# A list-building router beside linear attention: router steps, breaks on GpSimd and late gathers are moved

## The chip, the cores and the metric

The kernel runs on one core of one Trainium2 chip. The metric is the time of one execution on the device in microseconds. Three runs of the kernel before and one profiled execution of it are at hand. Everything is in fp32.

## The reference, cut to what matters

A gated linear attention (4 batches, 8 heads, 768 steps, 48 columns per head) is computed first. Its output, turned to 3072 tokens of 384 columns, goes through a router that picks 2 of 8 experts for each token, and through these experts.

```
f = 1 / (1 + exp(-f_logit))
for t in range(S):
    state = f[t] * state + k[t] (x) v[t]
    y[t] = q[t] . state
x = y as (3072, 384)
noisy = x @ w_gate + log1p(exp(x @ w_noise)) * noise
top2 = the two largest of noisy;  weights = softmax over the two
out[token] += weight * (relu(x[token] @ w1[e]) @ w2[e])      for both experts e
```

## The kernel before

**Attention stage.** The 768 steps are cut into 6 chunks (NCH) of 128 for each of the 4 batches, 24 blocks in all, which are done in 12 groups `g` of two blocks. Queries, keys and gates come in through a ring of buffers. TensorE turns q and k (`turn_q`, `turn_k`), makes the scores of the two blocks (`scores`, s = 0 and 1), VectorE masks them (A, L589), TensorE multiplies them with v (`within`), adds the carried state (`before`), turns the output into token rows (`features`), which SP stores to `x_rows` in DRAM. GpSimd multiplies and adds the carried state (`carried`: mid and st).

**Router and lists.** As soon as a chunk's logits are there, `route(c)` computes the two experts, their weights, and the place of each token in its expert's list. It is a generator: between its short VectorE, ScalarE and TensorE operations it yields, and the main loop takes a step or a few of it in each of its slots, so that a step's place in the engines' program order is set by the number of yields before it. The slots have names: "sc0" and "sc1" come after the two score halves, "y0" and "y1" after the two products with v. At the end of `route` there are 8 scatters for the chunk (`put`, L733), each an indirect DMA from GpSimd (POOL) that writes 128 list entries to `lists` in DRAM; 48 scatters in all. The main loop pops them one at a time. After each, `breath` puts a memset into POOL's queue: a tiny one (`spacer`), or, after every third, a break: a memset of one partition that is long in columns. In the chunks c = 0 to 4 (`c <= HALF + 1`, with HALF = 3) breaks are made; chunk 5 has none. In chunks 0 to 2 a break covers 2048 columns, later 768 and 576.

**Experts.** The work is cut into 10 items. Items 0 and 1 are the first 256 list entries (one "pair" of two blocks of 128) of experts 0 and 1; they use lists that are filled by chunks 0 to 2 and start within the attention stage. Items 2 and 3 are two further pairs of experts 1 and 0, items 4 to 9 three pairs each of experts 2 to 7. For each pair p:

- `fetch`: SP reads 256 list entries (4 KB) into `slots`. From pair 2 on this waits for all 48 scatters to land.
- `gather`: two indirect DMAs of POOL (s = 0 and 1, 128 rows each) read the token rows from `x_rows` into `xg` (4 buffers).
- For items 4 to 9, `stored` writes the 256 rows (384 KB) back to DRAM and `laid` reads them in another layout (4 DMAs of 96 KB), both on SP; then VectorE turns 32 x 32 blocks (STREAM_TRANSPOSE, L945). For the other items TensorE turns the rows (`xgp`, L949).
- the first layer, 8 pieces for each item (L1027 or L1166), the second layer, 7 pieces for each pair (y, L1332), and two scatters of POOL that add to the output (L1213). The turns for the next item sit in the second layer of the item ahead of it, in `between`.

The weights of an item (w1 and w2, 1.5 MB each) are loaded by SP; so are the weights for five further small blocks ("quarters", `w_q`, 1.5 MB for a load). The order on each engine is the order in which the program was written out, for SP and POOL too; `ahead(what, until)` issues the next fetches, stores, re-layouts and gathers up to a bound, from the loop over `pieces` at the end. Scatters of a pair wait for those of the pair ahead to land, since they add to the same rows.

In the second half of the kernel, a gather of a whole pair is issued at even pieces, wherever a pair's slots have been fetched, so some gathers stand between the scatters of the item that runs.

Of the kernel before, what the change touches and what calls it, by code (L numbers as in the profile page):

```python
# [332 lines left out]
def kernel(  # L333
# [94 lines left out]
    def two_banks(name):  # L428
        return ps2.tile([128, 2, 512], F32, tag="two", name=name)
# [142 lines left out]
    def turn_k(g, s):  # L572
        if s == 0:
            kT[g] = wk.tile([128, 2, HP * C], F32, tag="kT", name=f"kT_{g}")
            kT[g, "p"] = two_banks(f"kp_{g}")
        turn(kT[g, "p"][:, s], "k", g, s)
        if g == 0:
            nc.vector.tensor_copy(kT[g][:, s], kT[g, "p"][:, s])
        elif s == 1:
            nc.vector.tensor_copy(kT[g], kT[g, "p"])  # L580

    def scores(g, s):
        sc = sc_of[g, s] = two_banks(f"sc_{g}_{s}")
        for hp in range(HP):
            for par in range(2):
                nc.tensor.matmul(sc[:, par, cols(hp)], lhsT=kT[g][rows(par), s, cols(hp)],  # L586
                                 rhs=qT[g][rows(par), s, cols(hp)], start=True, stop=True)
        A[g, s] = wk.tile([C, 2, HP * C], F32, tag="A", name=f"A_{g}_{s}")
        nc.vector.tensor_tensor(A[g, s].rearrange("j r (a i) -> j (r a) i", i=C), sc.rearrange("j r (a i) -> j (r a) i", i=C),  # L589
                                causal.unsqueeze(1).broadcast_to((C, H, C)), ALU.mult)  # L590

    def carried(g):
# [11 lines left out]
        if c:  # L604
            mid = wk.tile([128, 2 * HP, D], F32, tag="mid", name=f"mid_{g}", bufs=1)
            nc.gpsimd.tensor_tensor(mid, ds, state[g % 2], ALU.add)
            ds = mid
        nc.gpsimd.tensor_tensor(new, ds, last, ALU.mult)
        state[g % 2] = new

# [47 lines left out]

    xs_of = {}

    def route(c):
# [26 lines left out]
        nc.vector.tensor_tensor(ex, mx[:, :, 0:2], mx[:, :, 0:1].broadcast_to((128, B, 2)), ALU.subtract)  # L688
        for _ in range(2):
            yield from pause()  # L690
# [19 lines left out]
        else:  # L710
# [3 lines left out]
                                     data1=each.rearrange("t e b -> t (e b)"), initial=0.0, op0=ALU.mult, op1=ALU.add)  # L714
        for _ in range((4, 5, 5, 17, 11, 8)[c]):
            yield from pause()
# [14 lines left out]
        def put(b, r):  # L731
            n_put.append(c)
            into = nc.gpsimd.indirect_dma_start(  # L733
                out=lists, out_offset=bass.IndirectOffsetOnAxis(ap=sloti[:, r, b:b + 1], axis=0),
                in_=entry[:, c, b, r, :], in_offset=None)
            tc.declare_no_dep(into.ins, group="lists", reason="slots differ")
            tc.add_to_no_dep_group("lists", into.ins)
            if c >= HALF:
                tc.declare_no_dep(into.ins, group="full", reason="slots differ")
                tc.add_to_no_dep_group("later", into.ins)  # L740
            breath(c <= HALF + 1)

        puts.extend([partial(put, b, r) for b in range(B) for r in range(2)])
        yield


    in_a_row = [0]

    def breath(broken):
# [3 lines left out]
        elif len(n_put) <= HALF * B * 2:  # L753
            nc.gpsimd.memset(spare[0:1, :], 0.0)
        else:
# [917 lines left out]
    for i in range(-3, NG):  # L1673
        for what in chain(back(i), front(i)):
# [17 lines left out]
            elif i == NG - 1 and what in ("x0", "x1", "f"):  # L1692
                zeros(4)
            for _ in range(6 if n_routed == NCH else 2 if n_routed == HALF + 1 else 3 if n_routed == NCH - 1 and i == NG - 1 else 1):
                next(router, None)
# [16 lines left out]
            if what == ("L0" if through(i + 2) or i == NG - 1 else "y1") and (i >= 2 and i % 2 == 0 or i == NG - 1):  # L1712
# [6 lines left out]
                if c == NCH - 1:  # L1719
                    router = chain(router, plan(), beyond())  # L1720
        if i < 0:
            warm_up(4)
# [19 lines left out]
    for item, piece in pieces:  # L1742
# [4 lines left out]
        if piece % 2 == 0 or item < NE - 1 and piece > 8:  # L1747
            ahead("laid", first_of[min(item + 2, len(items))])
            ahead("stored", done["gather"])
            ahead("gather", min(done["gather"] + 1, p + 4 if item < NE - 1 else first_of[min(item + 2 + (item >= NE), len(items))]))  # L1750
        n = item - NE - 2
# [60 lines left out]
```

## Time and profile before

| | |
|---|---|
| three runs | 620.51, 620.44, 618.16 us; median 620.44 |
| profiled execution | 621.6 us, span 619.8 us |
| TensorE (PE) busy | 599.9 us, 97% of the span |
| VectorE (DVE) | 455.8 us, 74% |
| ScalarE (ACT) | 279.8 us, 45% |
| GpSimd (POOL) | 246.8 us, 40% |
| mean granted TensorE clock | 0.989 of full speed |

The span runs from the first to the last instruction of the profile; the execution's own time has 1.8 us around it. A busy TensorE is not one at its peak: each fp32 matmul takes several passes. The span falls into the attention stage (to about 145 us), the first two items (to 195) and the other items.

### The profile page before, as it was taken

The numbers are of one execution on the slowest core, as the hardware profiler recorded it, in microseconds if no ns is written. First come the engines' busy times: TensorE is split into PE (matmuls) and PEld (weight loads), VectorE is DVE, ScalarE is ACT, GpSimd is POOL, SyncE is SP. The second block draws the span as 40 slices with busy tenths as digits, with TensorE's granted clock in tenths as the row PEclk, the third lists the DMA queues.
The fourth block names the chain that finished last, engine by engine and source line by source line (L and its number), as shares of the span: only waits on it lengthen the run. The fifth ranks groups of instructions, "written<-read, shape, count | busy, mean of one in ns | idle before, by whom it ended". The sixth has DMA issues, their size and how long they took to land.

```text
span 619.8 us, 12902 instructions
## 1 busy us (share of the span) xinstructions
PE 599.9 (97%) x4767; PEld 539.3 (87%) x4767; DVE 455.8 (74%) x1032; ACT 279.8 (45%) x715; POOL 246.8 (40%) x260
## 2 busy tenths in 40 slices
PE   8999999999969999999999999999999999999995
PEld 7788888777959998998898899889988898998994
DVE  6559778776735758898887878778788877887840
ACT  5766665532113323247316621761374247317611
POOL 3213299898864342151153224322433152323032
PEclk9999999998988999999999999999999999999998
DMA  9999999969345679868866795769576949661024
GB/s 181 172 198 197 214 199 194 217 184 355 117 114 146 163 143 212 173 149 232 223 139 200 187 227 109 212 173 212 124 223 166 250 98 271 138 140 23 0 27 55
DMA packets 184511, 104.71 MB, mean 169 GB/s; under 512 B 144284, under 2 KB 177564, under 8 KB 184440
## 3 DMA queue, kind: packets, MB, share of 16 engines
q1 hardware_dynamic: 172392, 84.46, 53.4%
q0 software_dynamic: 12048, 19.35, 17.3%
q8 instruction: 39, 0.64, 0.4%
q14 instruction: 32, 0.26, 0.2%
HBM read 76.80 MB, written 27.23 MB: 168 GB/s over the span
## 4 chain that ended last, share of the span: by engine, by line
PE 79%; POOL 7%; DMA 7%; issue 2%; DVE 2%; SPq 1%; ACT 1%; POOLq 0%; ACTq 0%; DVEq 0%
PE y L1332 29%; PE D L1166 7%; PE E L1166 7%; PE C L1166 5%; PE B L1166 5%; POOL lists L733 5%; DMA out_dram<-ys,slots 2%; PE sc L617 2%; PE sc L586 2%; PE A L1166 2%; PE P L1027 2%; PE L L541 1%; SPq L523 1%; PE qp L563 1%; DMA xg<-x_rows,slots 1%
## 5 line engine op out<-in xcount | busy, mean ns | idle before, releaser
L1213 POOL DMA_INDIRECT out_dram<-ys,slots x48 | 79.9, 1664 | 175.5 <-DVE ys L1338 102.6
L1332 PE MATMUL y<-q_all,f_all 128*128 128x192 f32 x528 | 94.7, 327 | 1.4 <-ACT ys L1348 1.4
L1332 PEld LDWEIGHTS y<-q_all,f_all 128*128 128x128 f32 x528 | 86.6, 190 | 2.1 <-ACT ys L1348 1.7
L895 POOL DMA_INDIRECT xg<-x_rows,slots x48 | 49.5, 1032 | 72.7 <-DMA slots<-lists 31.9
L1332 PE MATMUL y<-w,hs_b 128*128 128x192 f32 x352 | 64.4, 326 | 0.0
L733 POOL DMA_INDIRECT lists<-entry,sloti x48 | 52.5, 1094 | 20.1 <-DVE mx L683 11.0
L1338 DVE SCALAR_TENSOR_TENSOR ys<-y,slots,ys 128x192 f32<-128x192 f32 x66 | 27.4, 415 | 44.2 <-PE y L1332 16.5
L1332 PEld LDWEIGHTS y<-w,hs_b 128*128 128x128 f32 x352 | 58.4, 190 | 0.4
L1174 ACT ACTIVATE hs_b<-hs_b 128x256 f32<-128x256 f32 x120 | 50.1, 418 | 8.3 <-DVE hs_b L1178 7.2
L1381 ACT ACTIVATE ys<-y,slots 128x192 f32<-128x192 f32 x22 | 9.3, 422 | 96.9 <-PE y L1332 96.9
L589 DVE TENSOR_TENSOR A<-sc,causal 128x1024 f32<-128x1024 f32 x24 | 28.7, 1219 | 12.3 <-PE sc L586 12.2
L1332 PE MATMUL y<-w,f_all 128*128 128x192 f32 x176 | 32.7, 329 | 0.0
L1332 PE MATMUL y<-q_all,hs_b 128*128 128x192 f32 x176 | 32.7, 329 | 0.0
L1332 PEld LDWEIGHTS y<-q_all,hs_b 128*128 128x128 f32 x176 | 28.9, 190 | 2.1 <-issue 2.1
L1201 DVE TENSOR_TENSOR f_all<-hs_b 128x512 f32<-128x512 f32 x44 | 30.0, 685 | 0.0
L1332 PEld LDWEIGHTS y<-w,f_all 128*128 128x128 f32 x176 | 28.9, 190 | 0.8
L1166 PE MATMUL C<-v_all,ws_b 128*128 128x256 f32 x96 | 28.7, 380 | 0.1
L586 PEld LDWEIGHTS sc<-qT,kT 64*128 64x128 f32 x384 | 22.5, 188 | 6.4 <-issue 3.5
L1171 ACT COPY hs_a<-D 128x256 f32<-128x256 f32 x66 | 24.5, 370 | 7.2 <-PE D L1166 5.4
L617 PEld LDWEIGHTS sc<-A,v_all 128*64 128x64 f32 x384 | 20.6, 137 | 6.2 <-DVE A L589 4.2
L617 PE MATMUL sc<-A,v_all 128*64 128x128 f32 x384 | 24.5, 277 | 1.0 <-DVE A L589 1.0
L586 PE MATMUL sc<-qT,kT 64*128 64x128 f32 x384 | 24.9, 279 | 0.6 <-DVE mx L683 0.6
(277 smaller groups left out, 1413.0 us busy)
## 6 DMA issues: line engine op xcount, KB each, us to landing
w<-in_moe_w_dram SPq DMA_DIRECT2D x40, 384.0 KB
w_q<-in_moe_w_dram SPq DMA_DIRECT2D x10, 1536.0 KB
w<-in_moe_w_dram SPq DMA_DIRECT2D x6, 1536.0 KB
rows_of<-xg SPq DMA_DIRECT2D x18, 384.0 KB
v_all<-in_v_dram SPq DMA_DIRECT2D x12, 384.0 KB
x_rows<-xs SPq DMA_DIRECT2D x12, 384.0 KB
out_dram<-zero SPq DMA_DIRECT2D x24, 192.0 KB
k_all<-rows_of SPq DMA_DIRECT2D x48, 96.0 KB
```

Source lines behind the costliest of these rows:

```text
L586: nc.tensor.matmul(sc[:, par, cols(hp)], lhsT=kT[g][rows(par), s, cols(hp)], rhs=qT[g][rows(par), s, cols(hp)], start=True, stop=True)
L589: nc.vector.tensor_tensor(A[g, s].rearrange("j r (a i) -> j (r a) i", i=C), sc.rearrange("j r (a i) -> j (r a) i", i=C), causal.unsqueeze( ...
L617: nc.tensor.matmul(at(g, s, h), lhsT=slot_of("v", g)[:, s, h, :], rhs=A[g, s][:, h % 2, cols(h // 2)], start=(j < 2), stop=(g < 2 and j >= ...
L733: into = nc.gpsimd.indirect_dma_start(out=lists, out_offset=bass.IndirectOffsetOnAxis(ap=sloti[:, r, b:b + 1], axis=0), in_=entry[:, c, b, ...
L895: nc.gpsimd.indirect_dma_start(out=xg[p][:, s, :], out_offset=None, in_=x_rows[0:HALF * B * C] if p < NE else x_rows, in_offset=bass.Indir ...
L1166: nc.tensor.matmul(banks[name, j], lhsT=half_of(x, k)[:, j * 128:(j + 1) * 128], rhs=half_of(y, k), start=first, stop=True, skip_group_che ...
L1171: nc.scalar.copy(at(to, j), banks[more[0], j])
L1174: nc.scalar.activation(at(to, j), at(y, j), AF.Relu, scale=-1.0 if more[0][0] == "-" else 1.0)
L1201: nc.vector.tensor_tensor(sm[which], x, y, op)
L1213: into = nc.gpsimd.indirect_dma_start(out=out, out_offset=bass.IndirectOffsetOnAxis(ap=slots[p][:, s, 2:3], axis=0), in_=ys[s], in_offset= ...
L1332: nc.tensor.matmul(to, lhsT=x[:, o, :], rhs=y[:, o, :], start=(start and o == 0), stop=(o == FH - 1), skip_group_check=not start)
L1338: nc.vector.scalar_tensor_tensor(to, in0=bank, scalar=gate[s], in1=to, op0=ALU.mult, op1=ALU.add)
```

## The change

Four things are changed. In the main loop the router takes no step in the slot "sc0", and twice the usual number in "y0"; in chunk 3 eight of its pauses are moved from after the running count to ahead of the exponential. Breaks: they are 1400 columns in chunks 0 to 2, chunk 5 has them too, and `carried` starts the count of three again. At the start, the two halves of the first group's turned keys get a bank each in place of one tile of two banks, and four warm-up matmuls are left out. In the loop over pieces, from item 2 on, a gather is issued by halves in pieces 1 to 8, one half for each piece, in place of a whole pair at even pieces.

```
     def turn_k(g, s):
         if s == 0:
             kT[g] = wk.tile([128, 2, HP * C], F32, tag="kT", name=f"kT_{g}")
-            kT[g, "p"] = two_banks(f"kp_{g}")
+            if g:
+                kT[g, "p"] = two_banks(f"kp_{g}")
+        if g == 0:
+            p = one_bank(f"kp_0_{s}")
+            turn(p, "k", 0, s)
+            nc.vector.tensor_copy(kT[0][:, s], p)
+            return
         turn(kT[g, "p"][:, s], "k", g, s)
-        if g == 0:
-            nc.vector.tensor_copy(kT[g][:, s], kT[g, "p"][:, s])
-        elif s == 1:
+        if s == 1:
             nc.vector.tensor_copy(kT[g], kT[g, "p"])
...
         nc.gpsimd.tensor_tensor(new, ds, last, ALU.mult)
+        in_a_row[0] = 0
         state[g % 2] = new
...
-        for _ in range(2):
+        for _ in range(10 if c == HALF else 2):
             yield from pause()
         nc.scalar.activation(ex, ex, AF.Exp)
...
-        for _ in range((4, 5, 5, 17, 11, 8)[c]):
+        for _ in range((4, 5, 5, 9, 11, 8)[c]):
             yield from pause()
...
-            breath(c <= HALF + 1)
+            breath(True)
...
         elif len(n_put) <= HALF * B * 2:
-            nc.gpsimd.memset(spare[0:1, :], 0.0)
+            nc.gpsimd.memset(spare[0:1, 0:1400], 0.0)
...
-            for _ in range(6 if n_routed == NCH else 2 if n_routed == HALF + 1 else 3 if n_routed == NCH - 1 and i == NG - 1 else 1):
+            steps = 2 if n_routed == HALF + 1 else 3 if n_routed == NCH - 1 and i == NG - 1 else 1
+            for _ in range(6 if n_routed == NCH else 0 if what == "sc0" else 2 * steps if what == "y0" else steps):
                 next(router, None)
...
-        if i < 0:
+        if i < -1:
             warm_up(4)
...
         if piece % 2 == 0 or item < NE - 1 and piece > 8:
             ahead("laid", first_of[min(item + 2, len(items))])
             ahead("stored", done["gather"])
-            ahead("gather", min(done["gather"] + 1, p + 4 if item < NE - 1 else first_of[min(item + 2 + (item >= NE), len(items))]))
+        if item >= NE:
+            if 1 <= piece <= 8 and done["gather"] < min(done["fetch"], first_of[min(item + 3, len(items))]):
+                gather(done["gather"], (1 - piece % 2,))
+                done["gather"] += 1 - piece % 2
+        elif piece % 2 == 0 or item < NE - 1 and piece > 8:
+            ahead("gather", min(done["gather"] + 1, p + 4 if item < NE - 1 else first_of[item + 2]))
```

## Rows read from the trace of the kernel before

**Rows 1.** The page: the busy time of each engine, and the group of the list scatters (count | busy us, mean ns of one | idle us before them).

```profile
PE 599.9 (97%) x4767; PEld 539.3 (87%) x4767; DVE 455.8 (74%) x1032; ACT 279.8 (45%) x715; POOL 246.8 (40%) x260
...
L733 POOL DMA_INDIRECT lists<-entry,sloti x48 | 52.5, 1094 | 20.1 <-DVE mx L683 11.0
```

**Rows 2.** The waits of TensorE, the longest in total: what waited, for whom, us in total, times, longest us.

```profile
PE xgp L949 <- DMA xg<-x_rows,slots: 6.6, 2, 5.2
```

**Rows 3.** Windows: from:to and length in us, then the busy time of PE, PEld, DVE, ACT and POOL (with instructions), the mean granted TensorE clock, the share of the DMA engines, GB/s.

```profile
0.00:27.00 27.00, 24.67 (x266) 20.39 (x268) 15.39 (x30) 16.34 (x31) 4.96 (x24) 1.00 0.91 178
...
136.00:146.00 10.00, 8.67 (x97) 6.39 (x96) 4.38 (x16) 2.38 (x6) 8.79 (x14) 0.83 0.84 254
...
180.00:191.00 11.00, 6.03 (x27) 5.94 (x28) 1.38 (x4) 1.77 (x5) 5.49 (x5) 0.69 0.95 302
191.00:600.00 409.00, 407.53 (x2559) 375.14 (x2558) 324.48 (x704) 180.29 (x501) 125.03 (x92) 1.00 0.67 161
```

**Rows 4.** The chain that ended last, around the second pair's gather: start us, us, what.

```profile
172.78 4.71 DMA lists<-entry,sloti
177.51 2.73 DMA slots<-lists
...
181.03 3.80 DMA xg<-x_rows,slots
...
184.97 0.87 PE xgp L949 x3
```

**Rows 5.** The timeline of POOL in the first half of the list scatters (start us, us, engine, line, operation, out<-in; in brackets the idle time before it and what ended it): a scatter, a break and the scatter behind it, and scatter 25.

```profile
96.53 0.96 POOL L733 DMA_INDIRECT lists<-entry,sloti  x1 [0.22 <-issue]
97.48 1.79 POOL L754 MEMSET hs_a<- 1x2048 f32 x1
99.44 0.96 POOL L733 DMA_INDIRECT lists<-entry,sloti  x1 [0.17 <-issue]
...
129.11 1.54 POOL L733 DMA_INDIRECT lists<-entry,sloti  x1 [0.16 <-issue]
```

**Rows 6.** The same of chunks 4 and 5: scatters 38 to 41, 44 and 48, with a break between the first two.

```profile
158.21 1.01 POOL L733 DMA_INDIRECT lists<-entry,sloti  x1 [0.22 <-issue]
...
160.74 0.96 POOL L733 DMA_INDIRECT lists<-entry,sloti  x1 [0.17 <-issue]
...
162.01 0.96 POOL L733 DMA_INDIRECT lists<-entry,sloti  x1 [0.22 <-issue]
...
163.27 0.96 POOL L733 DMA_INDIRECT lists<-entry,sloti  x1 [0.22 <-issue]
...
167.06 1.63 POOL L733 DMA_INDIRECT lists<-entry,sloti  x1 [0.22 <-issue]
...
172.78 2.52 POOL L733 DMA_INDIRECT lists<-entry,sloti  x1 [0.23 <-issue]
```

**Rows 7.** The timeline of VectorE: the casts that end the routing of chunks 3 and 5, and two subtractions of weights.

```profile
123.78 0.17 DVE L729 CAST sloti<-slot 128x8 uint32<-128x8 f32 x1 [0.18 <-DVE slot L728]
...
155.54 0.17 DVE L729 CAST sloti<-slot 128x8 uint32<-128x8 f32 x1
...
172.06 0.94 DVE L974 TENSOR_TENSOR q_all<-w,q_all 128x768 f32<-128x768 f32 x1
...
173.53 0.94 DVE L974 TENSOR_TENSOR q_all<-w,q_all 128x768 f32<-128x768 f32 x1
```

**Rows 8.** The timeline of TensorE: the second half of group 9's products with v, which waits for its mask.

```profile
116.59 1.09 PE L617 MATMUL sc<-A,v_all 128*64 128x128 f32 x16 [0.69 <-DVE A L589]
```

**Rows 9.** The chain that ended last, at the start.

```profile
9.91 7.59 DMA k_all<-in_k_dram
...
20.61 5.55 DMA f_all<-in_f_logit_dram
```

**Rows 10.** Around TensorE's one stop among the late items, in item 7: two lines of the chain (the second layer's first products; a scatter to the output until it landed), and the timelines of SP (weight loads) and of TensorE.

```profile
468.77 2.60 PE y L1332 x16
...
482.06 10.61 DMA out_dram<-ys,slots
...
481.08 1.79 SPq L920 DMA_DIRECT2D w<-in_moe_w_dram  x4
...
483.45 0.40 SPq L1408 DMA_DIRECT2D w_q<-in_moe_w_dram  x1
...
493.33 1.57 PE L1332 MATMUL y<-q_all,f_all 128*128 128x192 f32 x8 [1.41 <-ACT ys L1348]
```

**Rows 11.** The timelines in item 5, which begins at 328 us: SP's two weight loads, POOL's last scatter of item 4 and the next gather, the start of the second layer on TensorE, and VectorE's transposes of item 6's first two pairs.

```profile
331.48 0.49 SPq L923 DMA_DIRECT2D w<-in_moe_w_dram  x1
...
332.65 0.38 SPq L1406 DMA_DIRECT2D w_q<-in_moe_w_dram  x1
...
342.71 1.57 POOL L1213 DMA_INDIRECT out_dram<-ys,slots  x1 [6.55 <-ACT hs_a L1171]
349.01 1.01 POOL L895 DMA_INDIRECT xg<-x_rows,slots  x1 [4.73 <-DMA slots<-lists]
...
354.10 1.46 PE L1332 MATMUL y<-w,hs_b 128*128 128x192 f32 x8
...
362.02 0.97 DVE L945 STREAM_TRANSPOSE xt_a<-k_all 128x768 f32<-128x768 f32 x1
...
367.33 0.97 DVE L945 STREAM_TRANSPOSE xt_a<-k_all 128x768 f32<-128x768 f32 x1
```

More of the change, by code (lines that the diff above doesn't have):

```diff
@@ L590, in scores @@
                                 causal.unsqueeze(1).broadcast_to((C, H, C)), ALU.mult)
+    in_a_row = [0]
     def carried(g):
@@ L657, in turned_logits @@
                                 p.rearrange("t s (r w) -> t s w r", r=HP)[:, :, 0:2 * E], axis=AX.X, op=ALU.add)
-    xs_of = {}
     def route(c):
@@ L740, in put @@
                 tc.add_to_no_dep_group("later", into.ins)
-            breath(c <= HALF + 1)
+            breath(True)
         puts.extend([partial(put, b, r) for b in range(B) for r in range(2)])
         yield
-    in_a_row = [0]
     def breath(broken):
```

## The prediction

> **What bounds the kernel now.** I read the page's busy times first. TensorE is busy 599.9 us of the 619.8 us span [rows 1], so an edit that shortens work on another engine can pay at most the 20 us in which TensorE stands still, and what its clock loses around those gaps. Next I read what TensorE waited for [rows 2] and the windows by stage [rows 3]. The attention stage starts with some gaps under its first loads. Then there are two sore places: 136 to 146 us, where 1.3 us are idle and the mean granted clock is 0.83 of full speed, and 180 to 191 us, where 5 us are idle and the clock is 0.69. From 191 to 600 us TensorE is idle only 1.5 us in 409. Its longest wait is for gathered rows (xg) [rows 2].
>
> Last I read the chain through the second sore place [rows 4]. Backwards: the transposes of pair 2 wait for the gather of its rows (3.80 us), that for its slots out of the lists (2.73), and that for the last list scatter to land: it starts at 172.78 us and lands 4.71 later, at 177.49. From there to TensorE's restart at 184.97 are 7.48 us that the change leaves alone. Before them POOL runs scatters and breaks end to end [rows 5, 6], from its first scatter to the 48th. So in this stage the time is set by POOL's queue, and what the change is worth here is how much earlier scatter 48 lands. TensorE cannot eat that up: it stands still 5.2 us before the restart [rows 2].
>
> **The first half's breaks.** I counted POOL's order through the loop for both versions. Before, chunks 0 to 2 have 8 breaks of 2048 elements. After, the counter starts again behind each carried state, so there are 6 breaks of 1400. A broken step takes 2.91 us from scatter to scatter (96.53 to 99.44 [rows 5]), an unbroken one 1.26 (162.01 to 163.27 [rows 6]), so a break costs 1.65. The memset is 1.79 us of it [rows 5]; at 1400/2048 of that, 1.22 (an estimate), a new break costs 1.08. POOL saves 8 x 1.65 - 6 x 1.08 = 6.7 us and could start scatter 25 at 122.4 us in place of 129.11. It may not: chunk 3's slots are written by VectorE only at 123.78 + 0.17 = 123.95 us [rows 7], and the change to chunk 3's pauses (8 fewer late, 8 more early) leaves that cast at the same place of VectorE's order. So scatter 25 starts at 124.0: **5.1 us earlier**, the rest is lost in a wait. Behind it POOL stays the bound: chunk 4's and 5's slots are early enough (chunk 5's at 155.7 [rows 7], its first scatter at 163.27 [rows 6], some 158 after).
>
> **The last chunk's breaks.** In chunk 5, scatters 41, 44 and 47 get a break. With one, a step takes 2.53 us (158.21 to 160.74), without 1.26 [rows 6], so three add **3.8 us**, straight in the chain. Two scatters of this chunk are long now: number 44 takes 1.63 us and number 48 takes 2.52, against 0.96, together 2.23 over. What breaks do to that no row of before shows. Bounds: all 2.23 stays, or all goes. While number 48 runs, VectorE does two subtractions of two SBUF operands, to 174.47 us [rows 7]; such overlaps come by chance of timing, and over all 48 scatters the mean is 1.09 us [rows 1], 0.13 over the usual, or 1.1 for eight. I take that mean, nearer to how such overlaps fall than either end: 2.2 becomes 1.1, **1.1 us gained**.
>
> The Trainium skill, "SBUF — State Buffer", in its section on the two sides of SBUF, says that VectorE and GpSimd share a port pair under an exclusive lock, which a VectorE instruction with two SBUF inputs takes against a GpSimd instruction that reads SBUF; whoever starts first holds it to its end. Number 48 fits it. By that rule a break, which only writes, could run while VectorE holds the pair, and the scatters behind it would be free of it: 2.2 gained in place of 1.1.
>
> **The router's steps.** Steps issued after the first half of the scores move behind the first half of the products, so that the second mask is not queued behind two maxima. That mask holds TensorE 0.69 us at 116.59 [rows 8]. It may bring chunk 3's slots, and so scatter 25, forward by 0 to 0.7 us; I take 0, since POOL's own queue is then close behind. Elsewhere the moved steps are short and wait for nothing new. The edits at the start (kp in two one-bank tiles, 4 fewer warm-up matmuls) cost and bring nothing: until 26 us the chain runs through loads, k of 7.59 us and f of 5.55 [rows 9]. Without that cover no more than the 2.3 us for which TensorE is idle there [rows 3] could be gained, and a lower clock after fewer warm-up matmuls could cost as much.
>
> The first gathers, of pair 0, also come 5.1 us earlier and take away the wait and the slow clock around 140 us (some 3 us of TensorE's time [rows 3]). That is worth nothing by itself: TensorE only comes earlier to the wait at 180 us. **List stage: 5.1 - 3.8 + 1.1 = 2.4 us, bounds 1.3 and 5.1 - 3.8 + 2.2 + 0.7 = 4.2.**
>
> **Late gathers by halves.** From item 2 on, gathers leave their places between the scatters and go into pieces 1 to 8 of the item before the one that uses them. The count of instructions and bytes is the same. On POOL the scatters no longer queue behind gathers that wait for slots (349.01, 4.73 us of waiting [rows 11]). What can that bring? TensorE is stopped once: at 493.33 for 1.41 us, by ScalarE, which waits for the buffer of a scatter issued at 482.06 [rows 10]. That one took 10.61 us to land, while SP had just issued two weight loads, at 481.08 and 483.45 [rows 10]. Before the first of them in SP's queue stands the re-layout of a pair that is gathered late. After the change it stands ahead of that and can go out when the first layer ends, at 468.77 [rows 10], 12 us earlier. **I take the 1.4 us as gained**; bounds 0 and 1.4.
>
> What is late next: SP's store and re-layout of each pair. SP now stores pair 12 (item 5, for instance) when item 5 has begun, and the weights for item 7 are issued ahead of the re-layout of pair 13. VectorE's transposes want the first pair at 362.02 and the second at 367.33, 7.9 and 13.2 us after the second layer begins at 354.10 [rows 11]. POOL's last scatter of the item before goes out at 342.71 now, 14 us into the item, with gathers in its way, so six gathers end there some 8 us later, and stores and re-layouts fill the rest. The re-layout of pair 13 waits for 1.5 MB of weights issued from 354.1 on. Two such loads and the slots behind them took 331.48 to 349.01 [rows 11], 8.8 us each; the re-layout's own 0.4 MB adds some 2 at that rate, so it lands near 366: a margin of about 1 us. I take no stall.
>
> The Trainium skill speaks against this part: "DMA: Bandwidth & Descriptors", section on queues, rings and completion order, has each DMA engine consume the descriptors of a ring in order, so small copies of SP wait out the weights before them. The 4.73 us wait of the gather at 349.01 for a 4 KB fetch agrees.
>
> **Sum:** 2.4 + 1.4 = 3.8 us off the profiled execution, 621.6 us (span 619.8): 617.8. Its own time is 1.2 us over the median of 620.44, so on that scale **616.6 us**. About 0.5%, 3.1 us, is what a measurement of this kernel tells from no change.
>
> **Rivals.** (a) *The last chunk's breaks eat the gain*: the long scatters stay long, POOL meets some in the first half too, and the gap at 493 us stays or moves. Gain 1.3 us or less: 619.1. For it: 3.8 of 5.1 us are certain costs on the chain. Against: a mean excess of 0.13 us. Chance 0.25. (b) *Late re-layouts stall VectorE and through it TensorE*, slower: items 4 to 8 turn pairs of a blocked item. The point is 13.2 us after the second layer's start; if the second re-layout lands 1.5 us behind it in each of the five, that is 7.5 us, less 2.4: 625.5. For it: the margin of 1 us. Against: weights and scatters go out earlier too, and now the first re-layout is done well before 362. Chance 0.15. (c) *The breaks shield the scatters*: they run beside VectorE's two-operand work, every scatter of chunk 5 is short, and the mask brings 0.7: 4.2 + 1.4 = 5.6 us, 614.8. For it: number 48. Against: a break is as likely to end in such work as to cover it. Chance 0.10. The lock of the Trainium skill's "SBUF — State Buffer" would make it so. My forecast has 0.50; its own range is 614.8 to 619.1.
>
> **Range and chances.** 613.0 to 621.0 us holds the forecast, (a) and (c), with 1.2 us for the spread of the runs before (618.16 to 620.51), and leaves out (b) and little else. Faster by over 0.5% means below 617.3: 0.36 of the forecast's 0.50, with (c) and some of the spread, 0.48. Slower: (b) and 0.01, 0.16. Between: 0.36.
>
> **What would show it.** Right: scatter 25 on POOL at 124 us, six memsets of 1400 at about 1.2 us, no wait on xg near 140; scatter 48 landing 2 to 3 us earlier and the restart 7.5 us behind it; scatters of chunk 5 at 0.96 us beside three breaks; no wait on a scatter's landing near 490. Wrong: scatter 25 held beyond 125 by chunk 3's slots or scatters that are long again; scatter 48 landing after 176; stream transposes waiting for re-laid rows, and TensorE gaps after 250 us.

## The result: half a per cent slower

The changed kernel takes 621.88 us (median of 22 runs), the kernel before 619.95 us beside it: a ratio of 1.0055, 95% interval 1.0037 to 1.0073. The medians are 1.9 us apart, the ratio makes 3.4 us: the ratios here and below leave out runs more than 1.5% above the fastest one of the same kernel (6 of 22 of the kernel before, none of the changed one), so they lie above the quotients of the medians, here 1.0031. The predicted range, to 621.0 us, doesn't reach the measured time. The profiled executions are 2.1 us apart (own time 623.72 us against 621.6, span 622.0 against 619.8).

The windows of the changed kernel, as in [rows 3]:

```profile
0.00:27.00 27.00, 24.35 (x264) 20.37 (x264) 15.91 (x30) 16.81 (x31) 4.97 (x24) 1.00 0.94 184
...
136.00:146.00 10.00, 10.00 (x120) 7.80 (x118) 6.22 (x24) 3.37 (x9) 8.68 (x15) 1.00 0.85 239
...
180.00:191.00 11.00, 7.62 (x38) 7.51 (x39) 1.62 (x5) 1.44 (x3) 4.86 (x5) 0.69 1.00 305
191.00:600.00 409.00, 404.14 (x2534) 371.35 (x2533) 322.67 (x699) 179.45 (x499) 127.00 (x92) 1.00 0.67 160
```

The sore place at 136 to 146 us is gone. The one at 180 is a little smaller (7.62 us busy against 6.03) and its clock is still 0.69. The loss stands in the last line: from 191 to 600 us TensorE is busy 404.14 us, where it was 407.53 [rows 3]. Its waits say for what (as in [rows 2]):

```profile
PE xgp L952 <- DMA xg<-x_rows,slots: 5.9, 1, 5.9
PE y L1335 <- DVE ys L1341: 4.7, 2, 3.2
PE rk L723 <- DVE each L710: 1.7, 1, 1.7
```

The second wait is new. Before, one stop of 1.41 us stood there [rows 10]; now there are two, and they cost 3.3 us more than it did. The third is new as well: TensorE waits for chunk 3's counts.

In the list stage, POOL's timeline answers to [rows 4 to 6]: a break of the first half, scatter 25, scatters 44, 47 and 48, the gather of pair 2; then TensorE's restart.

```profile
115.79 1.26 POOL L757 MEMSET hs_a<- 1x1400 f32 x1
...
125.42 1.01 POOL L738 DMA_INDIRECT lists<-entry,sloti  x1 [3.78 <-DVE sloti L734]
...
164.85 1.63 POOL L738 DMA_INDIRECT lists<-entry,sloti  x1 [0.22 <-issue]
...
170.54 2.55 POOL L738 DMA_INDIRECT lists<-entry,sloti  x1 [0.22 <-issue]
...
174.61 0.96 POOL L738 DMA_INDIRECT lists<-entry,sloti  x1 [0.17 <-issue]
...
179.38 1.00 POOL L898 DMA_INDIRECT xg<-x_rows,slots  x1 [1.61 <-DMA slots<-lists]
```

```profile
183.38 0.88 PE L952 MATMUL xgp<-ident,xg 128*128 128x128 f32 x3 [5.86 <-DMA xg<-x_rows,slots]
```

A short break takes 1.26 us (the estimate was 1.22). Scatter 25 starts 3.7 us earlier than before, not 5.1. Scatter 48 starts at 174.61, 1.8 us *later* than its 172.78 [rows 6], because three breaks stand ahead of it and the two long scatters are as long as they were (1.63 and 2.55; the second is now number 47). TensorE restarts at 183.38 in place of 184.97: 1.6 us earlier. So in the profiles 1.6 us are won, 3.3 us lost; that makes 1.7 of the 2.2 us between the two spans.

### The profile page after: what moved, and what is told of

Same layout as the page of the kernel before. It is cut to its first block, busy times and chain, and to the rows that moved or that the text cites. A ratio compares the mean times of both kernels' runs of the same rounds, so it can differ in the third digit from the quotient of the medians.

```text
span 622.0 us, 12895 instructions
## 1 busy us (share of the span) xinstructions
PE 598.0 (96%) x4759; PEld 538.0 (87%) x4759; DVE 460.2 (74%) x1032; ACT 280.0 (45%) x715; POOL 244.5 (39%) x263
## 5 line engine op out<-in xcount | busy, mean ns | idle before, releaser
L1216 POOL DMA_INDIRECT out_dram<-ys,slots x48 | 81.8, 1704 | 201.1 <-DVE ys L1341 122.4
L1335 PE MATMUL y<-q_all,f_all 128*128 128x192 f32 x528 | 94.3, 327 | 0.0
L1335 PEld LDWEIGHTS y<-q_all,f_all 128*128 128x128 f32 x528 | 86.7, 190 | 0.3
L1335 PE MATMUL y<-w,hs_b 128*128 128x192 f32 x352 | 64.4, 326 | 0.0
L1335 PEld LDWEIGHTS y<-w,hs_b 128*128 128x128 f32 x352 | 58.4, 190 | 0.4
L1335 PE MATMUL y<-w,f_all 128*128 128x192 f32 x176 | 33.0, 331 | 4.8 <-DVE ys L1341 4.7
L1335 PEld LDWEIGHTS y<-w,f_all 128*128 128x128 f32 x176 | 28.7, 190 | 6.5 <-DVE ys L1341 5.7
L1335 PE MATMUL y<-q_all,hs_b 128*128 128x192 f32 x176 | 32.7, 329 | 0.0
L1335 PEld LDWEIGHTS y<-q_all,hs_b 128*128 128x128 f32 x176 | 28.9, 190 | 2.1 <-issue 2.1
```

The lines of the kernel that those rows point to most:

```text
L1216: into = nc.gpsimd.indirect_dma_start(out=out, out_offset=bass.IndirectOffsetOnAxis(ap=slots[p][:, s, 2:3], axis=0), in_=ys[s], in_offset= ...
L1335: nc.tensor.matmul(to, lhsT=x[:, o, :], rhs=y[:, o, :], start=(start and o == 0), stop=(o == FH - 1), skip_group_check=not start)
```

## Experiments

Kernels were run on five chips, each time with the kernel before beside them; ratios are to that one. The kernel before took 616.9 to 619.0 us on three of the chips and 623 to 624 us on two. On these two, all profiles show idle time of TensorE that nothing in the trace ends, and several conclusions come out the other way; they are taken last, except for one kernel that is marked.

**The late gathers, both ways.** First the changed kernel with the old line for the gathers, and the kernel before with the new ones alone:

```
-        if item >= NE:
-            if 1 <= piece <= 8 and done["gather"] < ...
...
+            ahead("gather", min(done["gather"] + 1, p + 4 if item < NE - 1 else first_of[min(item + 2 + (item >= NE), len(items))]))
```

> The changed kernel with the late gathers put back as they were (whole pairs, where the kernel before had them); the router's steps, the pauses, the breaks stay changed. Theory 1 (the late gathers lose the time: two stops of TensorE for y, 3.16 + 1.54 us, in place of one of 1.41; the list stage gains 1.6): the two stops go, the one of 1.4 near 493 comes back, and the kernel is 1.6 us faster than the one before, about 618.3, ratio 0.997. Theory 2 (the loss sits in the router's steps and the breaks, the late stops are covered elsewhere): as slow as the changed kernel, 621.5 or more, ratio 1.003 to 1.006. Theory 3 (the stops in the late items move about with any shift of the stage before them): some stop for y of 1 to 5 us at another place, ratio 0.998 to 1.004.

> The kernel before with the late gathers by halves alone. Theory 1: the list stage is that of before (gather of the first late pair near 181.0, TensorE going on near 185.0), and the late items lose 4.70 - 1.41 = 3.3 us: about 623.2, ratio 1.005, with VectorE waiting for a re-laid pair 5 us near 483 to 490. Theory 2: the late items lose nothing, 618.5 to 620, ratio 0.998 to 1.000.

Measured: 618.8 us (kernel before 618.97; 1.0026, 0.9996 to 1.0055) without them, and 622.06 (1.0075, 1.0034 to 1.0115) with them alone. By medians the late gathers alone cost 3.1 us, near the 3.3 of the changed kernel's profile; between the changed kernel and the one without them the medians differ by 3.1 us too (not taken side by side; by the ratios it is 1.8 us). So theory 1 holds for its second half, by the times. Its first half doesn't: the rest of the change wins nothing. And the trace of the late gathers alone doesn't show 3.3 us. VectorE does wait for re-laid pairs in it, as theory 1 said, but TensorE loses no more by it than the 1.41 us of before, and in the window from 191 to 600 us it is busy 407.55 us, as it was (407.53 [rows 3]):

```profile
DVE xt_a L945 <- DMA k_all<-rows_of: 5.5, 2, 3.0
PE y L1332 <- DVE ys L1338: 1.4, 2, 1.0
```

So the loss is shown by the times of these runs; that it comes by VectorE's wait is read from the changed kernel's profile and is not shown for every run. Theory 3, stops that move about, isn't excluded either: its range holds the kernel without late gathers.

**What lies in the rest.** On that chip, two more kernels with old late gathers: breaks out of the last chunk again (`breath(c <= HALF + 1)`), and chunk 3's pauses back to 2 and 17.

> The changed kernel with old late gathers, and without the three breaks of 1.30 us in the last chunk's scatters. Theory 1: the breaks stand on POOL's path and shield nothing (the two long scatters of 1.63 and 2.55 us are there with them as without), so the first late gather comes 3.9 us earlier, near 175.5, and the time is 614 to 615, ratio 0.991. Rival (breaks shield the scatters): without them the eight scatters of the last chunk cost 2 to 4 us more, the gather is within 1.5 us of 179.4, and the time is within 1.5 us of the run with old late gathers.

> The changed kernel with old late gathers and chunk 3's pauses as before (2 ahead of the exponential and 17 ahead of the ranks, not 10 and 9). Theory 1: the new pauses make chunk 3's slots late (scatter 25 waited 3.78 us for them and began at 125.42); with the old ones it begins near 124.0, and the first late gather comes 1.4 us earlier: 617, ratio 0.995. Rival (scatter 25's start is made good by the slots of the later chunks): the gather stays near 179.4 and the time is that of the run with old late gathers, ratio 0.997.

Without the last chunk's breaks: 613.17 us (0.9929, 0.9903 to 0.9955), 5.6 us below the run that has them. POOL's timeline of that kernel, scatters 45 and 48, the scatter to the output and the gather of pair 2, and its window:

```profile
164.93 1.65 POOL L738 DMA_INDIRECT lists<-entry,sloti  x1 [0.22 <-issue]
...
169.42 0.96 POOL L738 DMA_INDIRECT lists<-entry,sloti  x1 [0.22 <-issue]
170.75 3.11 POOL L1216 DMA_INDIRECT out_dram<-ys,slots  x1 [0.29 <-issue]
174.22 1.01 POOL L898 DMA_INDIRECT xg<-x_rows,slots  x1 [0.37 <-issue]
```

```profile
180.00:191.00 11.00, 10.24 (x61) 9.54 (x61) 7.00 (x19) 3.08 (x7) 3.52 (x3) 1.00 0.75 207
```

Scatter 48 starts 5.2 us before that of the changed kernel (169.42 against 174.61) and the gather follows it 4.8 us behind in both. Three breaks of 1.30 us are 3.9 of the 5.2. The rest is the second long scatter: without breaks the list is finished when VectorE's subtractions (L977) come for the second time, and what is held then is the scatter to the output (3.11 us), behind the last list scatter. The breaks pushed scatter 47 into those subtractions. From 180 to 191 us TensorE now works 10.24 of 11 us at full clock. Theory 1's 3.9 us hold; that the long scatters stay on the list's path with breaks as without doesn't.

The old pauses: 619.86 us (1.0037, 1.0003 to 1.007), scatter 25 at 125.85 after a wait of 4.10 us. Theory 1 of that run falls; the pauses aren't what makes the slots late. Its TensorE stops twice for y among the late items, though it has the old late gathers (`PE y L1335 <- ACT ys L1351: 3.1, 2, 1.8`), so such stops do move. VectorE's and POOL's timelines of the changed kernel show what makes the slots late, and those of the kernel before (the last three lines) how it was:

```profile
119.08 1.69 DVE L693 TENSOR_TENSOR ex<-mx 128x8 f32<-128x8 f32 x1
121.04 0.62 DVE L699 SCALAR_TENSOR_TENSOR sm<-ex 128x4 f32<-128x4 f32 x1 [0.27 <-ACT ex L696]
```

```profile
118.72 0.96 POOL L738 DMA_INDIRECT lists<-entry,sloti  x1 [0.22 <-PE qp L563]
...
119.73 1.00 POOL L612 TENSOR_TENSOR mid<-ds,st 128x384 f32<-128x384 f32 x1
120.81 0.83 POOL L614 TENSOR_TENSOR st<-mid,ending 128x384 f32<-128x384 f32 x1
```

```profile
119.09 0.16 DVE L688 TENSOR_TENSOR ex<-mx 128x8 f32<-128x8 f32 x1
119.53 0.16 DVE L694 SCALAR_TENSOR_TENSOR sm<-ex 128x4 f32<-128x4 f32 x1 [0.28 <-ACT ex L691]
...
126.33 0.99 POOL L606 TENSOR_TENSOR mid<-ds,st 128x384 f32<-128x384 f32 x1
```

Two small instructions of the router, 0.16 us each in the kernel before, end with POOL's two operations for the carried state (120.77 with 120.73, 121.66 with 121.64). POOL's shorter breaks moved those operations under the router of chunk 3; before they came behind it, at 126 us. So chunk 3's slots are written at 125.1, not 123.95 [rows 7]. The run with old pauses shows the same two (1.69 and 0.62 us).

**Which part brings the gain.** The kernel before with one part each, in the order short breaks, router's steps with pauses, start:

```
-            nc.gpsimd.memset(spare[0:1, :], 0.0)
+            nc.gpsimd.memset(spare[0:1, 0:1400], 0.0)
```

```
+            steps = 2 if n_routed == HALF + 1 else 3 if n_routed == NCH - 1 and i == NG - 1 else 1
+            for _ in range(6 if n_routed == NCH else 0 if what == "sc0" else 2 * steps if what == "y0" else steps):
```

```
-        if i < 0:
+        if i < -1:
             warm_up(4)
```

> The kernel before with the shorter breaks of the first half alone, once more. On a chip where the kernel before takes about 619 us and TensorE has no unexplained idle time in the attention stage: Theory A (these breaks are the 5.8 us that the change gains beside its losses) 0.991 to 0.994; Theory B (scatter 25 is then held by chunk 3's slots, and it takes the router's steps too) 0.996 to 0.999. Where the kernel before takes 623 us or more: 1.003 to 1.007, as in the two runs there.

> The kernel before with the router's steps and chunk 3's pauses alone, once more. On a chip where the kernel before takes about 619 us: Theory A 0.999 to 1.001 (scatter 25 stays near 129), Theory B 0.996 or less. Where the kernel before takes 623 us or more: 1.000 to 1.007, as in the run there.

> The kernel before with the two edits at the start alone (banks of their own for the first two turned keys, and no filling products in the step before the first group). Theory A: the start waits for its first loads whatever TensorE does, so nothing: within 0.5 us of the kernel before. Theory B: the missing filling products leave TensorE's clock low for longer, 1 us or more slower; or the separate banks let the first group begin earlier, 1 us or more faster.

Short breaks alone: 612.54 us beside 616.93 (0.9944, 0.9909 to 0.9980). Router's steps alone: 615.22 us (0.9989, 0.9958 to 1.0020). Start alone, on one of the two chips taken last: 623.35 us beside 624.0 (1.0007, 0.9969 to 1.0046). The times lie nearest to theory A each time. POOL's timeline with the short breaks alone, scatters 25 and 48 and the gather:

```profile
124.81 1.00 POOL L736 DMA_INDIRECT lists<-entry,sloti  x1 [3.04 <-DVE sloti L732]
...
168.69 0.96 POOL L736 DMA_INDIRECT lists<-entry,sloti  x1 [0.22 <-issue]
...
173.82 1.01 POOL L897 DMA_INDIRECT xg<-x_rows,slots  x1 [0.68 <-issue]
```

Scatter 25 is 4.3 us earlier than in the profile of the kernel before, the gather 7.2, of which 5.7 come from scatter 48: it starts 4.1 us earlier, ahead of VectorE's second subtractions, and takes 0.96 us, not 2.52 [rows 6]. But the profile with the router's steps alone, a change that brings no time clear of noise, has much of this too:

```profile
127.23 1.02 POOL L733 DMA_INDIRECT lists<-entry,sloti  x1 [1.80 <-DVE sloti L729]
...
171.12 0.96 POOL L733 DMA_INDIRECT lists<-entry,sloti  x1 [0.22 <-issue]
...
175.98 1.01 POOL L895 DMA_INDIRECT xg<-x_rows,slots  x1 [0.42 <-issue]
```

Scatter 25 isn't near 129 there, as theory A had it, and the gather is 5.0 us earlier than before. (Both profiles begin their first list scatter earlier than that of the kernel before, at 70.82 and 69.96 against 72.62 us.) And on this chip 7 of the 21 runs of the kernel before took 610.8 to 614.6 us, the others 616.2 to 621.0; with the short breaks all 10 took 610.9 to 614.3. So the gain of 4.4 us by medians is shown by the times, but the short breaks reach nothing that the kernel before doesn't reach in a third of its runs, and with one profile of the kernel before (621.6 us) the traces can't say what differs between its runs. Whether scatter 48 falls under the subtractions is a likely reading, not a shown one.

By medians the parts are -4.4 us for these breaks, +5.6 for the last chunk's and +3.1 for the late gathers, +4.3 in all, where 1.9 was measured; by the ratios they are -0.6, +1.0 and +0.7%, 1.2% in all, where 0.55% was. The signs agree, but parts taken on different chips and in different company give the whole to 2 or 3 us and no better.

**Why the late gathers are late.** From here all kernels have the quiet last chunk. Late gathers as changed; then with the next expert's weights given out behind the re-layouts (`owed.append(k + NR + 1)` for the `ahead(1, k + NR + 1)` of items 2 on, and in the loop):

```
+        if piece == 10 and owed:
+            ahead(1, owed.pop())
```

then, instead, with more pieces allowed: `1 <= piece <= 20` for `1 <= piece <= 8`.

> The changed kernel without breaks in the last chunk's scatters: all of the change but that part, late gathers by halves included. Adding up (the late gathers cost a fixed 3.1 us wherever the list stage ends): 613.2 + 3.1 = 616.3, ratio 0.998. If the cost of the late gathers hangs on how the list stage ends (items 4 us earlier against the same transfers): 613 to 614.5 or over 618.

> As the run with late gathers by halves and a quiet last chunk, with the next expert's first matrix (four transfers of 384 KB) given out three pieces later, behind the re-laid pairs in SP's order, as the kernel before had it. Theory 1a (the second pair's re-layout lands late, and VectorE waits 5 us, because 1.5 MB of weights stand ahead of it in the queue): VectorE's wait of 5 us near 481 goes, the stop of 3.2 us of TensorE with it, and the time is 613.2 to 614.3, ratio 0.994. Theory 1b (the gathers themselves come too late, whatever stands ahead): the wait stays at 3 us or more, 616 or more, ratio 0.998.

> As the run with late gathers by halves and a quiet last chunk, with the halves allowed in pieces 1 to 20 of an item, not 1 to 8 alone, so that pairs are gathered in the item before, as far as their slots are there. Theory 1b (the bound to the first layer's pieces makes the pairs late, not the halving): VectorE's waits for re-laid pairs go, and the time is 613 to 614, ratio 0.993. Theory 1a alone, or halving itself costs (two more turns between the scatters on POOL): 616 or more.

Measured: 615.7 (0.9968, 0.9942 to 0.9993), 621.2 (1.0044, 1.0020 to 1.0067) and 612.52 us (0.9912, 0.9880 to 0.9945). The first is what adding up gave (616.3). The last is level with the quiet chunk and old late gathers on the first chip (613.17). So by medians the halving is free and the bound to pieces 1 to 8 costs 3.2 us; VectorE waits 4.8 us for re-laid pairs with the bound and 0.2 without. The two profiles don't show the 3.2 us: they are of 612.5 and 612.32 us, the first of them the lowest of runs that go up to 621.1, and TensorE's stops for y in it come to 0.7 us. The middle kernel is the instructive miss. Its waits of VectorE for pairs and TensorE's longest wait:

```profile
DVE xt_a L948 <- DMA k_all<-rows_of: 1.9, 2, 1.3
```

```profile
PE yp_q L1442 <- DMA w_q<-in_moe_w_dram: 3.5, 1, 3.5
```

VectorE's wait shrank as theory 1a had it (4.8 us in the run before, 8.6 in the changed kernel), but the 1.5 MB of weights now stand ahead of the quarter block's weights, and TensorE waits 3.5 us for those. In both orders of SP's queue that were tried something behind comes late; of these three kernels the one with earlier gathers is the one that doesn't pay for them.

**More of the same.** No breaks in the last two chunks (`breath(c <= HALF)`):

> The changed kernel with old late gathers and breaks neither in the last chunk's scatters nor in those of the chunk before it: three more breaks of 1.30 us are gone. Theory (breaks stand on POOL's path and shield nothing): the last scatter comes up to 3.9 us earlier, but TensorE's wait for the first late pair is only 1.9 us in the run with one quiet chunk, so the time falls by 1.5 to 2.5 us, to 611 to 612, ratio 0.989. Rival (breaks shield the scatters of a chunk that others work beside): scatters of the fifth chunk grow by 2 us or more in sum, and the time is 613 or more.

613.17 us (0.9923, 0.9886 to 0.9959), what one quiet chunk gave. The gather of pair 2 starts at 172.18 in place of 174.22, 2.0 us earlier, and has waited 2.75 us for the fetch of its list by then (0.37 with one quiet chunk). The theory's gain of 1.5 to 2.5 us isn't there. The rival's time is, but not for its reason: the fifth chunk's eight scatters take 8.6 us in sum, not more than with one quiet chunk (9.2). Part of POOL's gain is spent in waiting for the list to land and be fetched.

**Two chips on which it is otherwise.** These ran where the kernel before takes 623 to 624 us:

> The kernel before with the shorter breaks of the first half's scatters alone (1400 columns for 2048, and the count set back by the running sums' own work on POOL). Theory A (the 5.8 us that the change gains apart from the late gathers and the last chunk's breaks come from these breaks): scatter 25 begins near 124.0 to 124.5 in place of 129.1, the first late gather 5 us earlier, near 176, and the time is 613 to 615, ratio 0.991. Theory B (POOL gets ahead, but scatter 25 then waits for chunk 3's slots, which only the router's changed steps bring in time): scatter 25 begins at 126 or later, the time is 616 to 618, ratio 0.996.

> The kernel before with the router's steps and chunk 3's pauses alone. Theory A: POOL reaches scatter 25 at 129.1 as before, TensorE's stops of 0.7 us at the masks may go: 617.8 to 619, ratio 0.999 to 1.000. Theory B: the steps alone give 2 us or more, 616.5 or less, ratio 0.996. A loss of 1 us or more would say that the steps make TensorE wait for the ranks (1.7 us in the changed kernel) with nothing given back.

> The changed kernel with no breaks in the last two chunks' scatters, and late halves allowed in pieces 1 to 20: the two better settings together. If their gains add: the run with halves anywhere, 612.5, less at most 1.6 us that TensorE still waits there for the first late pair, 611 to 612.5, ratio 0.988 to 0.991. If the wait only moves to the next fetch of a list: 612.5 to 613.5.

> The changed kernel as it is, beside three others on one chip. Were the parts found so far additive there too, it stands at 1.0055 of the kernel before where TensorE has no unexplained idle time ahead of the list stage. On a chip where it has such idle time (the last four runs: the kernel before at 624), the router is late and sets the list stage, and the changed kernel stands at 1.008 or more, since the breaks' and gathers' prices stay and POOL's gain is lost.

> The changed kernel with old late gathers and no breaks in the last chunk's scatters. If POOL's chain sets the list stage: 0.992 to 0.994 of the kernel before, 8 us under the changed kernel. If the router's late slots set it (a chip with idle time in the attention stage): 0.998 to 1.003, since time saved on POOL is spent there waiting for the slots.

> The kernel before with the shorter breaks of the first half alone. Theory A (these breaks are the gain of the change): as the run with a quiet last chunk, 0.992 to 0.994. Theory B (scatter 25 then waits for chunk 3's slots, and what POOL gains it waits): 0.997 or more. In the run with a late router it was 1.0047, with a wait of 3.03 us for the slots at scatter 25.

> No breaks in the last two chunks, late halves in pieces 1 to 20. If the loss of the last run (1.0052) came from that chip's late router (POOL waited 4.64 us for the last chunk's slots): on a chip with a prompt router 0.988 to 0.992. If it comes from the two settings together: 1.003 or more again.

Measured in that order: 1.0047 (1.0012 to 1.0082), 1.0039 (0.9992 to 1.0086), 1.0052 (1.0009 to 1.0095), then on the other chip 1.0006 (0.9967 to 1.0044), 1.0114 (1.0073 to 1.0156), 1.0057 (1.0015 to 1.0098), 1.0069 (1.0030 to 1.0109). In us the medians are 624.96, 624.52 and 626.55 beside 624.0, then 623.25, 629.25, 626.72 and 626.40 beside 623.41. The forecasts for the changed kernel (1.008 or more), for the quiet last chunk (0.998 to 1.003) and the first one for the two better settings together (0.988 to 0.991) fail; the second one for those wasn't tested, since the router was late again (POOL waited 4.60 us for the last chunk's slots). Of the two runs with the short breaks alone the second lies where its theory B has it, the first above both theories. There the changed kernel is even with the one before, and the kernel with the quiet last chunk and old late gathers, 8.7 us under the changed kernel on the first chips by medians, is 6.0 us above it.

No profile of the kernel before is at hand from these chips, but eight of other kernels are (the start alone is the eighth), and three things differ in them. First, TensorE has idle time that nothing in the trace ends ("issue"), 2.4 to 8.0 us in sum in each of the eight and none in any of the twelve other profiles. Part of it lies in the attention stage; TensorE's timeline near 79 us, the changed kernel on one of these chips:

```profile
78.98 0.92 PE L604 MATMUL ds<-v_all,k_all 128*64 128x48 f32 x18
80.29 0.34 PE L604 MATMUL ds<-v_all,k_all 128*64 128x48 f32 x4 [0.38 <-issue]
81.02 0.30 PE L604 MATMUL ds<-v_all,k_all 128*64 128x48 f32 x3 [0.39 <-issue]
```

and in its first profile:

```profile
78.92 1.14 PE L604 MATMUL ds<-v_all,k_all 128*64 128x48 f32 x32
```

Most of the rest lies in the second layer of the quarter blocks: 2.4 to 4.0 us in the seven other kernels (as in the quiet kernel's line here) and 0.5 in the changed one.

```profile
PE yp_q L1441 <- issue: 2.8, 8, 0.5
```

Second, the routing is late: scatter 25 of the changed kernel starts at 130.94, not 125.42, again behind a wait of 3.77 us for chunk 3's slots, and chunk 5's slots are written at 162.9 to 165.8 us in the six kernels with short breaks. That isn't the chip alone: in the two without short breaks (router's steps, start) they are written at 155.2 and 157.8, near the 153.3 to 155.9 of all the other profiles. So on these chips the short breaks, which gain elsewhere, go with a late router; how one brings about the other is open. Third, in the last chunk VectorE stands still while POOL scatters without a break; the quiet kernel, POOL's last list scatter, VectorE, and TensorE behind it:

```profile
173.49 0.95 POOL L738 DMA_INDIRECT lists<-entry,sloti  x1 [0.22 <-issue]
```

```profile
174.81 0.35 DVE L1299 TENSOR_TENSOR ys<-P,y 128x192 f32<-128x192 f32 x1 [5.38 <-PE y L1279]
```

```profile
176.82 8.29 PE L1005 MATMUL hp<-xt_a,w 128*128 128x256 f32 x24 [3.10 <-DVE xt_a L953]
```

The product that VectorE is said to wait for was over by 169.5 us. TensorE then waits 3.10 us, and its 24 products take 8.29 us (granted clock 0.88 on the mean from 180 to 191 us), 5.34 in the changed kernel beside it: 6 us. (The two profiles are 9.4 us apart; some 5 of them are there when the list stage ends, the rest comes later, with the idle time in the quarter blocks.) All seven profiles from these two chips whose last chunk has no breaks show VectorE held there, for 1.9 to 5.4 us; the one that has them, the changed kernel, shows no such hold, nor does any profile from the other chips, though there too VectorE's sums of the second layer ran beside scatters without a break (160.2 to 164.5 us with the quiet last chunk). What holds VectorE isn't in the trace, and what TensorE's idle time comes from isn't either: both stay open. That the breaks prevent the hold is a likely reading of eight profiles, not a thing an experiment isolated. It also means that I can't name one version that beats both kernels everywhere: the kernel before with the short breaks alone is 4.4 us faster on one chip and 1.0 and 3.3 us slower on two others (by medians; by the ratios 0.6% faster, 0.5 and 0.6% slower).

## Why the prediction was wrong, step by step

- *What bounds the kernel*: right on the first chips. POOL's chain sets the list stage: without the last chunk's breaks the gather came 5.8 us earlier (180.01 to 174.22, same chip) and the time fell by 5.6. On the two chips taken last TensorE waits less than 0.5 us at a time for gathered rows in six of the eight profiles: there the late routing and VectorE set the stage.
- *The first half's breaks*, 5.1 us: right in kind, 3.7 us at scatter 25 in the changed kernel, 4.3 with the short breaks alone. The cast of chunk 3's slots was read off the trace as fixed at 123.95; POOL's own earlier operations delayed it by 0.6 to 1.6 us, on the clock of each trace (written at 124.53 with the short breaks alone, 125.14 in the changed kernel, 125.57 with the old pauses). The step didn't ask what moves under what when POOL gets ahead.
- *The last chunk's breaks*, 3.8 - 1.1 = 2.7 us lost: 5.6 by the times of two kernels. The 3.8 was right (3.9). The 1.1 for shorter scatters came out as nothing against the kernel before (1.63 and 2.55 us, where 1.63 and 2.52 stood), and as 1.6 us lost against the same kernel without breaks, whose list has one long scatter only. I took a mean over scatters for something with a place in time: VectorE's subtractions come when they come, and breaks that hold scatter 47 back put it under them. Taking queue time away ahead of them let that scatter through; adding some didn't.
- *The router's steps and the start*, nothing: right by the times (0.9989 and 1.0007, both with 1 inside the interval). Scatter 25 did come forward with the steps alone, by 1.9 us where 0 to 0.7 stood (in a profile whose first scatter is 2.7 us earlier already), without a gain clear of noise.
- *The late gathers*, 1.4 us won and no stall: this is the step that turned the sign. They cost 3.1 us by medians. That is rival (b) in kind, whose chance was 0.15 and whose price, 7.5 us, was too high. What failed is "a margin of about 1 us. I take no stall": VectorE waits for re-laid pairs in every profile with the bound to pieces 1 to 8 (1.9 to 8.6 us in sum), and hardly or not at all in the three with pieces 1 to 20. How much of it reaches TensorE varies: 4.7 us of stops in the changed kernel, 1.4 and 0.7 in the two other profiles named above, so the price is from the times, and its way to TensorE is shown for one execution. In that one the stop of 1.41 us did vanish. But the margin of 1 us for the second pair's re-layout was made from item 5, where POOL's last scatter of the item before goes out 14 us into the item. In item 7 a quarter block's scatter stands in that queue too. The changed kernel, item 7 from 440.9 us on: POOL's last scatter and the first and last of six gathers; SP's store of a pair, weights, re-layout; VectorE's transpose; TensorE's two stops.

```profile
460.17 1.55 POOL L1216 DMA_INDIRECT out_dram<-ys,slots  x1 [2.18 <-ACT hs_a L1174]
462.02 1.01 POOL L898 DMA_INDIRECT xg<-x_rows,slots  x1 [0.30 <-issue]
...
469.68 0.95 POOL L898 DMA_INDIRECT xg<-x_rows,slots  x1 [0.30 <-issue]
```

```profile
471.49 0.39 SPq L906 DMA_DIRECT2D rows_of<-xg  x1
471.97 3.46 SPq L923 DMA_DIRECT2D w<-in_moe_w_dram  x4
477.06 1.79 SPq L912 DMA_DIRECT2D k_all<-rows_of  x4
```

```profile
485.73 0.98 DVE L948 STREAM_TRANSPOSE xt_a<-k_all 128x768 f32<-128x768 f32 x1 [4.99 <-DMA k_all<-rows_of]
```

```profile
489.79 1.57 PE L1335 MATMUL y<-w,f_all 128*128 128x192 f32 x8 [3.16 <-DVE ys L1341]
...
539.70 1.57 PE L1335 MATMUL y<-w,f_all 128*128 128x192 f32 x8 [1.54 <-DVE ys L1341]
```

  The gathers start 21 us into the item, when the first layer is all but over, and the re-layout leaves SP at 477.06 and lands 8.7 us later, behind 1.5 MB. VectorE wanted it at 480.7. The order of the parts was foreseen; the start of the gathers was off by 7 us, against a margin of 1.
- *The rule of the Trainium skill* ("DMA: Bandwidth & Descriptors", queues, rings and completion order) that spoke against this part agrees with the runs: with the weights behind the re-layouts the wait went from them to the next load behind the weights.
- *The lock* of the Trainium skill ("SBUF — State Buffer", the two sides) was used to think of longer scatters only. By that page whoever starts first holds the pair to the end of its instruction. The trace has it the other way as well: VectorE's 0.16 us instruction takes 1.69, ending with POOL's sum. It fits the page in part only: the instruction begins under a scatter (118.72 to 119.68 us) but ahead of the sum (119.73), and is held by that too. As a rule for shielding, rival (c), it gave nothing.

## What to carry over

When an engine's queue is shortened, draw anew what its other operations now lie beside; a neighbour's date read off the old trace holds only while nothing moves under it. A margin worked out for one pass of a loop has to be worked out for the pass with the most in its queues. And an edit worth less than a per cent wants more than one chip: here the kernel without the last chunk's breaks was the best on one chip and the slowest on another. A part's worth measured by time should also be looked for in that part's own trace: two of the traces here don't show what the medians say.

## What the runs showed of the hardware

- VectorE and POOL held each other up, in both directions, until the other's instruction was over. VectorE's 0.16 us instruction took 1.69 us beside POOL's sum (119.08, above). POOL's scatter 47, at 170.54 for 2.55 us, ends 0.84 us after VectorE's last subtraction; scatter 44, at 164.85 for 1.63, 0.87 us after the first of two at 164.70. An undisturbed one takes 0.96.

```profile
164.70 1.82 DVE L977 TENSOR_TENSOR q_all<-w 128x768 f32<-128x768 f32 x2
...
169.84 0.94 DVE L977 TENSOR_TENSOR q_all<-w,q_all 128x768 f32<-128x768 f32 x1
...
171.31 0.94 DVE L977 TENSOR_TENSOR q_all<-w,q_all 128x768 f32<-128x768 f32 x1
```

- Chips differ by more than this change: the same kernel before took 617 us on one and 624 on another. What the difference consists of isn't shown, since the kernel before wasn't profiled there; every profile from the two slower chips has 2.4 to 8.0 us of TensorE's idle time that no record explains, every other profile has none.
